# The order and the engines of 1,943 operations, given by two tables of numbers

## The chip, the cores and the metric

The kernel runs on one core of a Trainium2 chip. The metric is the device time of one execution in microseconds; the time of a kernel is the median of several executions. Beside it stands one profiled execution, whose trace gives every duration below. The granted clock of TensorE was 1.0 throughout it.

The engines are named as in the profile: PE is TensorE's matmuls, PEld its weight loads, DVE is VectorE, ACT is ScalarE, POOL is GpSimd, SP is SyncE, whose queue issues most transfers.

## The reference

Two blocks follow each other. The first is attention with routing: every query and key gets the nearest of 16 centroids of its head, and a query attends only to keys of the same centroid. The second is a gated long convolution.

```python
# q, k, v: (4, 8, 768, 64); centroids: (8, 16, 64); all f32
q_assign = np.argmax(np.einsum('bhsd,hcd->bhsc', q_n, c_n), axis=-1)   # k_assign alike
mask = q_assign[:, :, :, None] == k_assign[:, :, None, :]
scores = np.where(mask, scale * np.matmul(q, k.transpose(0, 1, 3, 2)), -1000000000.0)
scores = scores - np.max(scores, axis=-1, keepdims=True)
attn = np.exp(scores)
attn = attn / (np.sum(attn, axis=-1, keepdims=True) + 1e-09)
x = np.matmul(attn, v)                  # -> (4, 768, 512), heads side by side
proj = x @ w_proj                       # (512, 1536)
x1, x2, x3 = (proj[..., :D], proj[..., D:2 * D], proj[..., 2 * D:])
x2_conv = np.fft.irfft(np.fft.rfft(x2, axis=1) * np.fft.rfft(filter_fft, axis=0)[None], n=S, axis=1)
return (x1 * x2_conv * x3) @ w_out      # (4, 768, 512)
```

## The kernel before

**The work.** The 32 pairs of batch and head are taken as 16 pairs of heads. Two pairs make a group n (8 groups, two for each batch element). For each group the kernel loads q and k, transposes them on PE (function `tr` and `tr2`, lines 594 and 607), copies them out of PSUM (line 282 on ACT, 284 on DVE and POOL: one helper, `copy`, serves all), casts them into the operands of the scores (tile `aug`), and works out the masks by a product with the centroids (line 627, or 512 for the first group), maxima and comparisons on DVE and a product with a triangle. The mask rows stand in the same operand tiles as extra rows of the contraction, so that the scores' product (line 84, tiles `aug`) already holds the mask. In the first group, functions named `put` copy the mask rows there on DVE (lines 557 and 284).

For each pair of heads there are six tiles of keys. Each gives three products of scores of 512 columns, three exponentials on ACT (lines 694 and 697), a weighted sum `pv` of eight matmuls (line 708) that accumulates in a PSUM pair, and a running sum of the exponentials for the denominator: line 725 (`part`, 512 columns, DVE or POOL) for the first two tiles, line 729 (`acc`, 1,536 columns, DVE) for the others. The sum over partitions is done by accumulating transfers on POOL's queue, or by a product (line 742) in the first groups and the last. Line 808 divides.

For each batch element the second block follows (`hyena`): the projection of x2 (line 843), sums and differences of its halves (857 and 862), the forward transform as products with a table `fw`, the product with the filter's spectrum (873 and 877), the inverse transform with a table `inv` (function `I`), sums and folds (944 and 954, function `fold`), the other two projections and their product (905 to 917), the gate (959) and the output projection (function `W`). For the last batch element, a sign-changed copy of `inv` is made on ACT (line 881), products of line 959 are split into two halves of the sequence for each of four blocks of columns, output tiles 0 to 2 need the one half and tiles 3 to 5 the other, and the projections of tiles 3 to 5 are split into three quarters of the contraction and the last quarter (that of tile 5 into two halves of its columns besides).

**The order.** No loop fixes the order of instructions. The function `build` lists 1,943 operations with a number (`seq`, in the order of the list), the engines that may run each with a price for every one, a due time, and what each reads and writes. A list scheduler (`place`) then puts them on the engines one by one. For each engine it takes those that are ready, works out when each could start, and of those that could start within 0.1 us of the earliest it takes the one with the least due time. Each operation goes to the engine at which it comes up first. The instructions are issued in the order of the starts that come out of it, and each engine runs its own in that order, waiting by semaphores for what they need. Operations of DVE and POOL marked `lock` (those that read and write SBUF on both) are kept apart: one on POOL waits for the one on DVE that was placed before it.

Two tables steer this. `NUDGE` adds a number to the due time of every operation, and `ONLY` pins an operation to one of its engines:

```python
        o.due += NUDGE.get(o.seq, 0.0)                         # line 99
...
            if o.seq in ONLY:                                  # line 183
                o.eng = {ONLY[o.seq]: o.eng[ONLY[o.seq]]}
...
                c = min((c for c in cand if c[0] <= t0 + wait + 1e-9), key=lambda c: (   # line 212
                    c[1].due - (bonus if e == "PE" and st.kind == "pv" == c[1].kind else 0.0)
```

Tiles in SBUF are held in fixed rings (5 tiles of exponentials, 3 sets of score operands, 4 of raw q and k, 3 of v); eight PSUM banks are given out by the same scheduler, two of them to the weighted sum.

Of the kernel before, what the change touches and what calls it, by code (L numbers as in the profile page):

```python
# [86 lines left out]
class Plan:  # L87
# [6 lines left out]
    def op(self, eng, fn, due, r=(), w=(), alloc=None, free=(), lock=False, byts=0, after=(), kind=None, lat=0.0, tab=None):  # L94
# [3 lines left out]
        o.seq = len(self.ops)  # L98
        o.due += NUDGE.get(o.seq, 0.0)
        o.outs, o.end, o.start, o.on = [], None, None, None  # L100
# [22 lines left out]
    def place(self, free0, banks_for, switch=0.1, wait=0.1, rate=RATE, bonus=0.0, margin=0.02195, shape=0.0):  # L123
# [58 lines left out]
        for o in self.ops:  # L182
            if o.seq in ONLY:
                o.eng = {ONLY[o.seq]: o.eng[ONLY[o.seq]]}
        for o in self.ops:
# [1098 lines left out]
```

## Time and profile before

| what | value |
|---|---|
| median of 3 runs | 371.18 us (371.1 to 372.21) |
| profiled execution | 370.64 us, its span 368.9 us |
| DVE's instructions, ACT's, POOL's | 478, 495, 162 |
| costliest group | line 708, 768 matmuls, busy for 143.0 us |
| DVE's costliest group | line 729, 64 instructions of 1.762 us |
| ACT's costliest group | line 697, 192 exponentials of 0.606 us |
| HBM | 106 GB/s over the span |

The span is the time from the first to the last instruction of the trace; the profiled execution's own time is that and what lies around it. Busy is the time in which an engine has at least one instruction; the idle time that stands with an instruction is that of its engine just before it, with what ended it.

### The profile page before, as it was taken

The page shows a single profiled execution, that of the slowest core. Times are in us where ns is not written, and L with a number is a line of the kernel's source. Part 1 is how long each engine was busy: PE and PEld are TensorE (multiplying, and loading weights), DVE is VectorE, ACT ScalarE, POOL GpSimd, SP SyncE. Part 2 cuts the span into 40 slices and gives each one's busy share as a digit, 9 for nine tenths or more (in the row PEclk, how much of TensorE's full clock was granted, in tenths as well). Part 3 has the DMA queues.
Part 4 walks back from the last instruction along what each step waited for, and adds up shares of the span by engine and source line. Part 5 has one row for each costly group of instructions (what it writes and reads, how often), then busy time and mean ns, then how long its engine had stood idle before and what let it go on. Part 6 is the DMA issues. An engine that isn't in the chain of part 4 may idle for free.

```text
span 368.9 us, 8653 instructions
## 1 busy us (share of the span) xinstructions
PE 357.5 (97%) x3314; PEld 208.9 (57%) x3316; DVE 342.5 (93%) x478; ACT 263.6 (71%) x495; POOL 120.9 (33%) x162
## 2 busy tenths in 40 slices
PE   7899999999999999999999999999999999999985
PEld 4455544555856565565555555566555655566672
DVE  7999999896999899999999999998998999999994
ACT  7998978877986859769869765899584785433242
POOL 7730730422032752331530044352221334016610
PEclk9999999999999999999999999999999999999999
DMA  7986597484247768748556964667477750110124
GB/s 175 202 189 126 128 211 195 93 189 110 62 80 156 115 156 169 152 103 129 107 64 183 238 170 81 146 152 98 81 116 167 150 77 1 48 45 2 59 115 171
DMA packets 90405, 46.20 MB, mean 125 GB/s; under 512 B 78248, under 2 KB 84092, under 8 KB 90364
## 3 DMA queue, kind: packets, MB, share of 16 engines
q1 hardware_dynamic: 85500, 36.15, 40.5%
q0 software_dynamic: 2752, 8.98, 17.1%
q10 hardware_dynamic: 2112, 0.52, 0.6%
q8 instruction: 26, 0.43, 0.5%
q14 instruction: 15, 0.12, 0.1%
HBM read 31.59 MB, written 7.40 MB: 106 GB/s over the span
## 4 chain that ended last, share of the span: by engine, by line
PE 78%; DVE 11%; ACT 5%; issue 3%; DMA 1%; POOL 1%; SPq 0%; DVEq 0%; ACTq 0%; POOLq 0%
PE bank L84 33%; PE pair L708 28%; PE bank L843 5%; PE bank L594 5%; DVE acc L729 3%; PE bank L627 2%; ACT p L697 1%; PE bank L82 1%; DMA qkraw<-in_k_dram 1%; DVE qkP L284 1%; PE bank L475 1%; PE bank L742 1%; ACT p L694 1%; PE bank L607 1%; DVE ohT L655 1%
## 5 line engine op out<-in xcount | busy, mean ns | idle before, releaser
L708 PE MATMUL pair<-p,vraw 128*64 128x385 f32 x768 | 143.0, 489 | 0.1
L697 ACT ACTIVATE p<-bank 128x512 f32<-128x512 f32 x192 | 108.7, 606 | 23.5 <-PE bank L84 16.0
L729 DVE TENSOR_TENSOR acc<-p,acc 128x1536 f32<-128x1536 f32 x64 | 112.8, 1762 | 3.2 <-ACT p L694 0.5
L84 PE MATMUL bank<-aug,aug 80*64 80x512 bf16 (+3 forms) x736 | 81.9, 327 | 2.1 <-ACT p L697 0.9
L708 PEld LDWEIGHTS pair<-p,vraw 128*64 128x64 f32 x768 | 56.6, 136 | 43.8 <-issue 36.7
L84 PEld LDWEIGHTS <-aug 80*64 80x64 bf16 (+1 forms) x736 | 45.6, 109 | 41.0 <-issue 26.3
L694 ACT ACTIVATE p<-bank 128x512 f32<-128x512 f32 x96 | 57.4, 606 | 5.4 <-PE bank L84 3.6
L284 POOL CAST aug<-qkP 64x768 bf16<-64x768 f32 x29 | 25.9, 900 | 83.3 <-DVE acc L729 55.9
L762 POOL DMA_DIRECT2D acc<-acc x30 | 24.4, 824 | 69.8 <-DMA acc<-acc 37.4
L84 PE MATMUL bank<-xT,wpj 128*64 128x384 bf16 x504 | 47.2, 326 | 0.0
L84 PEld LDWEIGHTS <-wpj 128*64 128x64 bf16 x504 | 30.2, 110 | 14.1 <-issue 2.6
L282 ACT COPY qkP<-bank 128x512 f32<-128x512 f32 (+1 forms) x46 | 23.1, 559 | 15.9 <-PE bank L594 9.7
L84 PEld LDWEIGHTS <-y 128*64 128x64 bf16 x472 | 24.0, 110 | 13.2 <-issue 3.6
L725 POOL TENSOR_TENSOR acc<-p,p 128x512 f32<-128x512 f32 x15 | 19.3, 1297 | 32.3 <-DVE acc L729 10.4
L873 DVE TENSOR_TENSOR tm<-bank,hm 128x512 f32<-128x512 f32 x44 | 28.1, 681 | 1.9 <-POOL uv L862 0.8
L84 PE MATMUL bank<-wout,y 128*64 128x512 bf16 (+1 forms) x200 | 24.0, 371 | 1.1 <-DVE y L959 1.1
L282 ACT CAST aug<-qkP 64x768 bf16<-64x768 f32 x28 | 23.2, 830 | 1.0 <-DVE qkP L284 0.4
L843 PE MATMUL bank<-wpj,xT 128*64 128x512 bf16 x192 | 22.7, 379 | 0.4 <-ACT p L697 0.4
L725 DVE TENSOR_TENSOR acc<-p,p 128x512 f32<-128x512 f32 x33 | 21.6, 690 | 0.4 <-DMA dd<-acc 0.4
L877 POOL TENSOR_TENSOR y<-tm 128x512 bf16<-128x512 f32 x14 | 17.8, 1277 | 12.8 <-DVE tm L873 10.6
L732 ACT COPY osb<-pair 128x770 f32<-128x770 f32 x16 | 12.9, 806 | 10.8 <-PE pair L708 10.7
L594 PEld LDWEIGHTS bank<-ident,qkraw 128*128 128x128 f32 x144 | 15.6, 141 | 6.3 <-ACT p L694 2.4
(178 smaller groups left out, 435.7 us busy)
## 6 DMA issues: line engine op xcount, KB each, us to landing
vraw<-in_v_dram SPq DMA_DIRECT2D x16, 384.0 KB, 5.2
qkraw<-in_q_dram SPq DMA_DIRECT2D x30, 192.0 KB, 3.9
rb<-dr SPq DMA_DIRECT2D x30, 192.0 KB, 3.7
qkraw<-in_k_dram SPq DMA_DIRECT2D x28, 192.0 KB, 3.6
out_dram<-ob SPq DMA_DIRECT2D x9, 512.0 KB, 5.0
acc<-acc POOLq DMA_DIRECT2D x10, 384.0 KB, 4.8
acc<-acc POOLq DMA_DIRECT2D x10, 192.0 KB, 4.2
y<-in_moe_filter_fft_dram SPq DMA_DIRECT2D x4, 384.0 KB, 4.3
```

Source lines behind the costliest of these rows:

```text
L84: T.nc.tensor.matmul(out[64 * i:64 * i + 64], lhsT[:, 64 * i:64 * i + 64], rhs, start=start, stop=stop)
L282: T.nc.scalar.copy(out, in_)
L284: (T.nc.vector if e == "DVE" else T.nc.gpsimd).tensor_copy(out, in_)
L594: T.nc.tensor.transpose(bank(h.ids[i // 4])[:, ts(i % 4, 128)], raw(ss[i // NT], i % NT), T.ident[:, ::-1] if 3 <= i < NT else T.ident)
L694: T.nc.scalar.activation(o, ap(h).rearrange("p (a b) -> p a b", a=2), Act.Exp, scale=0.125)
L697: T.nc.scalar.activation(flat(s)[:, lo:lo + 512], ap(h), Act.Exp, scale=0.125)
L708: T.nc.tensor.matmul(o[64 * hp:64 * hp + 64, ch, :385], T.vraw[vs][:, hp, sk * D:(sk + 1) * D], T.p[slots[sk]][:, hp, 384 * ch:384 * ch + ...
L725: alu(e).tensor_tensor(o, x, y, op=Alu.add)
L729: T.nc.vector.tensor_tensor(T.acc[os], T.p[slots[sk]][:, :, :S], T.acc[os], op=Alu.add)
L762: op(("POOL", .8), lambda e, rows=rows: T.nc.gpsimd.dma_start(flat_()[:rows], flat_()[rows:2 * rows], accum_op=Alu.add), te, r=[], w=AK, b ...
L843: T.nc.tensor.matmul(ap(h)[64 * i:64 * i + 64], T.xT[xs][:, kt, c:c + 64], T.wpj[:, kt, DM:2 * DM], start=kt == 0, stop=kt == ND - 1)
L873: op(("DVE", .68), lambda e, i=i, cs=cs, r=r, h=h: T.nc.vector.tensor_tensor(T.tm[r][:, cs], ap(h), hmrow(i, (0, 2, 2, 3)[2 * r + cs]), op ...
```

## The change

The two tables get other numbers; nothing else in the kernel differs. `NUDGE` has 1,943 entries before and after, and all of them differ, by 36.8 us in the median of the absolute differences. `ONLY` has 134 pins before and 128 after: 38 are the same, 28 operations are pinned to another engine, 68 pins are gone and 62 are new. The operations, their transfers, their prices, the tiles and the rule of choice stay as they were; the order and the engines follow from the new numbers, as the scheduler works them out. The diff, cut to some of the entries:

```diff
-NUDGE = {
-29:6.171,51:18.728,52:-22.192,85:-189.385,86:-167.539,89:-195.153,1857:-23.832,
-1886:-370.386,1887:13.072,1888:-296.022,1889:-466.918,1902:-292.682,
-1903:-1955.286,1916:-293.904,1917:-296.037,
...
-ONLY = {
-72:"POOL",100:"DVE",1416:"ACT",1886:"DVE",1926:"SP",
...
+NUDGE = {
+29:-7.972,51:50.833,52:43.343,85:97.767,86:98.143,89:98.42,1857:-129.09,
+1886:-3763.992,1887:-38.825,1888:-1267.888,1889:-13.798,1902:-911.492,
+1903:9.788,1916:-1644.568,1917:30.108,
...
+ONLY = {
+44:"DVE",65:"DVE",72:"ACT",100:"POOL",1416:"DVE",1485:"POOL",1512:"DVE",
+1767:"DVE",1768:"DVE",1819:"ACT",1886:"POOL",1887:"DVE",1926:"ACT",
...
```

In the list, 29 is a load of the first q and k, 44 and 65 a mirror of the angles and a copy of transposed q or k, 51 and 52 a pair of sines, 72 and 100 casts into `aug`, and 85, 86 and 89 three of the four `put`. 1416 and 1819 are copies of the projection of x2, 1485, 1886 and 1887 folds, 1512 a copy of the inverse transform's result, and 1767 and 1768 sums of line 725. 1857 is the sign change of `inv`; 1888, 1902 and 1916 are gates of line 959 for output tiles 0 to 2 (the second to the fourth block of columns), and 1889, 1903 and 1917 those for tiles 3 to 5. 1926 is a store of an output tile. The due time of an operation is the number in the list plus its entry in `NUDGE`.

More of the change, by code (lines that the diff above doesn't have):

```diff
@@ L43 @@
-ONLY = {13:"POOL",14:"POOL",15:"POOL",16:"POOL",18:"POOL",30:"ACT",32:"SP",33:"SP",36:"SP",37:"SP",40:"ACT",41:"DVE",66:"ACT",69:"DVE",72:"POOL",73:"ACT",85:"DVE",86:"DVE",93:"DVE",94:"POOL",97:"DVE",99:"DVE",100:"DVE",101:"POOL",141:"DVE",153:"DVE",213:"ACT",226:"POOL",227:"POOL",233:"POOL",238:"POOL",244:"POOL",245:"DVE",253:"DVE",254:"ACT",257:"DVE",288:"DVE",357:"POOL",358:"DVE",359:"POOL",394:"ACT",404:"ACT",406:"DVE",407:"DVE",408:"POOL",409:"ACT",416:"POOL",417:"POOL",418:"POOL",427:"DVE",430:"ACT",461:"POOL",462:"DVE",463:"DVE",498:"DVE",525:"POOL",533:"POOL",549:"DVE",551:"ACT",555:"ACT",566:"DVE",589:"DVE",593:"POOL",594:"POOL",600:"DVE",604:"DVE",639:"DVE",691:"POOL",692:"ACT",693:"POOL",694:"POOL",696:"ACT",697:"ACT",698:"ACT",699:"POOL",700:"POOL",701:"DVE",711:"DVE",808:"POOL",809:"POOL",856:"DVE",858:"ACT",859:"ACT",861:"POOL",862:"POOL",867:"POOL",913:"DVE",915:"POOL",1002:"DVE",1005:"DVE",1018:"DVE",1067:"ACT",1070:"DVE",1072:"ACT",1075:"ACT",1077:"DVE",1146:"POOL",1147:"POOL",1152:"DVE",1153:"DVE",1154:"POOL",1156:"ACT",1164:"ACT",1168:"ACT",1201:"DVE",1313:"DVE",1315:"ACT",1369:"DVE",1416:"ACT",1421:"ACT",1426:"ACT",1448:"DVE",1457:"DVE",1516:"POOL",1600:"POOL",1601:"POOL",1607:"POOL",1608:"POOL",1609:"POOL",1610:"DVE",1621:"DVE",1812:"ACT",1875:"DVE",1886:"DVE",1919:"ACT",1920:"SP",1922:"DVE",1923:"SP",1926:"SP",1930:"SP",1933:"ACT",1934:"SP",1938:"SP",1942:"SP"}
@@ new lines @@
+ONLY = {14:"POOL",15:"POOL",16:"POOL",18:"POOL",29:"SP",30:"ACT",32:"SP",36:"SP",38:"SP",39:"ACT",40:"ACT",44:"DVE",50:"DVE",65:"DVE",72:"ACT",89:"DVE",93:"DVE",94:"POOL",100:"POOL",101:"POOL",143:"DVE",147:"DVE",149:"ACT",155:"DVE",176:"DVE",177:"POOL",178:"DVE",226:"POOL",227:"POOL",232:"DVE",233:"POOL",238:"POOL",239:"POOL",244:"POOL",253:"ACT",254:"DVE",405:"ACT",407:"DVE",408:"POOL",409:"DVE",410:"ACT",413:"ACT",415:"ACT",416:"ACT",417:"POOL",418:"POOL",429:"DVE",461:"DVE",463:"DVE",498:"ACT",508:"DVE",522:"POOL",524:"DVE",525:"DVE",532:"POOL",548:"DVE",559:"DVE",564:"DVE",570:"ACT",577:"DVE",592:"DVE",600:"DVE",604:"ACT",688:"ACT",689:"ACT",690:"ACT",692:"POOL",693:"ACT",694:"ACT",696:"ACT",699:"POOL",700:"ACT",701:"ACT",857:"DVE",858:"DVE",859:"DVE",861:"DVE",862:"ACT",869:"POOL",870:"ACT",879:"DVE",914:"POOL",915:"POOL",1031:"DVE",1032:"DVE",1047:"DVE",1054:"DVE",1061:"POOL",1067:"DVE",1072:"ACT",1094:"DVE",1095:"POOL",1147:"POOL",1153:"ACT",1154:"DVE",1155:"ACT",1156:"ACT",1164:"ACT",1165:"DVE",1167:"ACT",1168:"DVE",1199:"DVE",1314:"POOL",1315:"ACT",1368:"POOL",1369:"POOL",1416:"DVE",1421:"ACT",1426:"ACT",1448:"DVE",1485:"POOL",1500:"DVE",1512:"DVE",1607:"ACT",1608:"POOL",1622:"DVE",1767:"DVE",1768:"DVE",1819:"ACT",1886:"POOL",1887:"DVE",1909:"ACT",1920:"SP",1923:"SP",1926:"ACT",1933:"ACT",1941:"DVE",1942:"SP"}
```

2 lines of the change are left out of this document (1 added, 1 removed).

## The prediction

> **What bounds the kernel now.** I read the first table of the page, then a table by stretches of 10 us, then the waits of PE, the chain of waits, and the timelines of the first 35 and the last 20 us. The first table says which engines are full; its columns are engine, busy us (share), instructions:
>
> ```profile
> PE 357.5 (97%) x3314; PEld 208.9 (57%) x3316; DVE 342.5 (93%) x478; ACT 263.6 (71%) x495; POOL 120.9 (33%) x162
> ```
>
> PE is the bound and DVE stands close behind it. The table by stretches (stretch, its length, busy us of PE, PEld, DVE, ACT and POOL, then granted clock, DMA share, GB/s) shows where PE is not full:
>
> ```profile
> 0.00:10.00 10.00, 7.44 (x35) 4.08 (x35) 7.36 (x24) 7.34 (x13) 7.16 (x32) 1.00 0.79 177
> ...
> 240.00:250.00 10.00, 9.25 (x108) 6.65 (x104) 9.37 (x14) 9.50 (x18) 5.02 (x5) 1.00 0.68 153
> ...
> 330.00:340.00 10.00, 10.00 (x112) 6.41 (x108) 9.90 (x18) 3.29 (x8) 5.64 (x4) 1.00 0.01 2
> ...
> 350.00:360.00 10.00, 8.93 (x156) 7.08 (x154) 9.85 (x21) 4.29 (x9) 1.40 (x2) 1.00 0.26 107
> 360.00:370.00 10.00, 4.63 (x44) 2.08 (x40) 3.46 (x8) 2.52 (x5) 0.00 (x0) 0.98 0.42 157
> ```
>
> From 30 to 350 us PE's idle time adds up to only 2.5 us (0.66 in 30:40, 0.28, 0.15 and 0.04 in the three stretches from 60, 0.42 in 100:110, 0.05 in each of the two after it, 0.06 in 160:170, 0.75 in 240:250). But ends of matmuls are modelled, so busy hides short stalls. I therefore also added up columns: unhindered, eight matmuls of the weighted sum (line 708) start 1.295 us apart, and a pair of 512-column half matmuls 0.213. At those rates the matmuls between 30 and 350 us fill 303 of the 320 us, so 17 are lost there; 10.7 are lost before 30 us and 6.2 between 350 and 368.9. Those 34 us are all that another order can work on. Part of the 17 is this, in the chain of waits (start, us, what):
>
> ```profile
> 79.71 1.30 PE pair L708 x8
> 81.00 1.47 PE bank L594 x12
> 82.47 1.45 PE pair L708 x8
> ```
>
> The weighted sum costs 1.45 behind the transposes (full-width array) and 1.30 behind the half-array scores. The matmuls change the width of their array tiles 59 times; at 0.10 to 0.15 each that is 6 to 9 of the 17 us, and 8 to 11 are short stalls.
>
> The end of the kernel, in the timeline (start, us, engine, line, operation, count, idle time before it and what ended it):
>
> ```profile
> 356.92 1.00 POOL L954 TENSOR_TENSOR sim<-sd 128x384 f32<-128x384 f32 x1 [6.52 <-DVE sd L944]
> ...
> 359.22 5.41 PE L84 MATMUL bank<-wout,y 128*64 128x256 bf16 x54 [1.07 <-DVE y L959]
> ...
> 361.88 0.55 DVE L959 TENSOR_TENSOR y<-sim,qkP 128x384 bf16<-128x384 f32 x1
> ...
> 364.67 0.69 DVE L284 COPY ob<-bank 128x512 f32<-128x512 f32 x1 [1.90 <-PE bank L84]
> ```
>
> PE waits for a gated product (line 959), then runs nearly the whole output projection in one piece; the last product is ready at 362.43, PE ends at 364.63, and a copy and a store take the last 4.3 us.
>
> At the front, DVE builds the first masks without a break from 14.65 to 22.79, ACT is full from 14.42 to its table load, and the first exponential waits 0.41:
>
> ```profile
> 21.02 1.28 ACT L408 ACT_TABLE_LOAD   x1
> ...
> 22.93 0.60 ACT L697 ACTIVATE p<-bank 128x512 f32<-128x512 f32 x1 [0.41 <-PE bank L84]
> ```
>
> **The change part by part.** No operation is added or removed. All 1,943 due times move, by a median of 37 us in either direction. The kernel compares due times only among operations that could start within 0.1 us of the earliest, so most of these shifts decide nothing by themselves. The engine pins can be read directly. I matched them to the engine each operation ran on (the placement agrees with the trace: 29 casts of line 284 on POOL, 28 on ACT, 7 on DVE). 60 pins name another engine than before; 68 old pins go, and 35 of those operations had run on DVE.
>
> *Engine load.* At the rows' means (cast 0.54 DVE, 0.83 ACT, 0.90 POOL; 512-column copy 0.69 DVE, 0.59 ACT; line 725 sum 0.69 DVE, 1.30 POOL; mask step 0.55 DVE, 0.48 ACT; fold 0.55 DVE, 1.01 POOL) the 60 moves add 6.1 us to DVE and take 2.9 from ACT and 2.5 from POOL. DVE has 26.4 idle. The 35 freed operations can move the other way; their mean price on DVE is near 0.6, so a third of them leaving would give 7 back. I set the net at nothing, with bounds of minus 6 and plus 6 us of DVE work.
>
> *Front, before 35 us.* One first q/k load (due 6.5 to -7.7) is pulled ahead in SP's queue, past two others at about 0.65 us of issue each, which come that much later. Before the first score a mirror and a q/k copy go from ACT to DVE, a cast from POOL to ACT and a cast from DVE to POOL: DVE +0.56+0.55-0.54 = +0.57, ACT -0.51-0.49+0.83 = -0.17. ACT's last pair of sines (1.0 us, at 13.36) gets due times of 52 and 60 where it had -13 and 27, so it falls behind the casts and copies; the exponential's table load needs it, and the total ahead of the load stays the same. PE waits 0.9 for a load and 0.7 for a copy here, and 0.41 end before the first exponential: a gain of up to 2.0. A loss of up to 1.1, if two DVE instructions of 0.55 get ahead of the mask copies, whose due times rise from -180 to 107. I take **-0.5**, nearer the row of the shortest wait, because both engines have to get shorter for the first exponential to move.
>
> *Middle, 35 to 350 us.* The waits with a name are few: 0.9 us of PE for exponentials (three times), 0.7 for a mask, 1.05 lost in 246 to 248 us, where scores wait for exponentials behind a 0.87 us sign change of the inverse table on ACT. That one instruction gets a due time 105 us earlier (258 to 153), out of the way of a full ACT (9.50 of 10 in 240:250). Bounds: 0 to -4 from stalls, half of the 8 lost; +3 if half of DVE's 6.1 lands where DVE has no gap. I take **-1.2**: that stall and a little of the others.
>
> *End.* Output tiles 3 to 5 have their last quarter split off (0.22 us of PE each, half that for the two halves of tile 5); tiles 0 to 2 do not. Before, the products for tiles 0 to 2 had due times of 45 to 50 for the last three column blocks and came last, so four quarter-blocks and whole projections, 2.2 us, stood behind the last product. Now they get -569 to -1301, and the products for tiles 3 to 5 327 to 374. If those come last, 0.22+0.22+0.11+0.11 = 0.66 us of PE remains behind the last product: a gain of up to 1.5. One fold goes from DVE to POOL and another back; on POOL it costs 1.00 against 0.55, so 0.45 are lost if it stands in that chain. One store goes from SP's queue to ACT's, ahead of at most one copy; ACT waits 1.90 to 2.83 between copies there, which hides its issue (0.33), and it costs 0.33 without that cover. Bounds -1.5 and +0.6; I take **-1.0**, the gain less that 0.45.
>
> For the fold on POOL the row has 6.52 us of idle time ended by DVE. "SBUF — State Buffer" (Who interferes with whom) of the Trainium skill says that a DVE instruction with two SBUF inputs and a GpSimd instruction that reads SBUF shut each other out. The trace agrees as far as that row goes; by this rule the handover costs up to one more 0.55 us DVE instruction, and the end would be -0.45 instead of -1.0.
>
> *Sum.* -0.5 - 1.2 - 1.0 = -2.7. The profiled execution took 370.64 us (span 368.9 and 1.74 around it), so 367.94 for such a one; the median of the three runs is 0.54 above it, which gives **368.5 us**.
>
> **The rivals.**
> *A larger gain.* The front reaches its 2.0, the end its 1.5 and the middle 2: 371.2 - 5.5 = 365.7. For it: 34 us are lost in all. Against: DVE's chains at both ends keep their length. 0.15.
> *Nothing.* The stalls reappear elsewhere, since PE's work and the operations between the first load and the first exponential are the same: 371.2. 0.13.
> *DVE becomes the bound (slower).* After 290 us DVE is 9.6 to 10.0 of 10 busy, and the pins after 280 add: a tile copy 0.69, two sums 1.38, a copy 0.55, less a fold 0.55 and a copy 0.69, net +1.4. If the freed pins do not take that away, and the front and end gain nothing, the end comes at 371.2 + 1.4 = 372.6. It decides once DVE's queue, and not PE's, is what holds 300 to 350: idle time on PE there, ended by lines 873 or 917. Against: PE is at 10.00 there and had slack of one or two tiles. 0.16.
> *More changes of the array (slower).* Ten more than 59, at 0.15, with no gain elsewhere: 371.2 + 1.5 = 372.7. For it: the due times of transposes and scores lose their old grouping. Against: nothing shows that they get more scattered. 0.06. "TensorEngine Tiling (Array Packing)" (Key Properties) of the Trainium skill says that a change of tiling mode drains the engine; the 1.45 against 1.30 agrees.
>
> **How the numbers follow.** Forecast 0.50, larger gain 0.15, nothing 0.13, DVE 0.16, array 0.06. About 0.3%, or 1.1 us, is what a measurement here can tell from no change, so same means 370.1 to 372.3. Faster: 0.50 + 0.15 = 0.65, slower: 0.16 + 0.06 = 0.22, same 0.13. The likeliest case alone spans 367 to 370. The range reaches to the larger gain and to both slower rivals: 365.6 to 372.7.
>
> **What would show it.** In the changed profile: PE's busy time within 1 us of 357.5 and its idle time lower by 2 to 3; the first exponential between 21 and 23 us; no stall of PE near the sign change of the table (line 881); less than 1 us of PE behind the last product of line 959. It is wrong if PE shows idle time ended by DVE after 300 us, if the first exponential is later than 24, or if PE's busy time rises by over 1.5 us, which would be the array's changes.

## The result, and the profile after

The changed kernel takes 374.27 us in the median of 6 executions (373.12 to 375.03), the kernel before 371.12 beside it (370.98 to 372.21). The ratio is 1.0078, with a 95% interval of 1.0055 to 1.0101: slower by about 3 us, where 2.7 less was forecast, and 1.6 us above the upper end of the range. The profiled execution took 374.13 us, its span 372.4.

The first table of the page of the changed kernel (engine, busy us, share, instructions):

```profile
PE 361.2 (97%) x3319; PEld 215.0 (58%) x3319; DVE 340.0 (91%) x470; ACT 272.6 (73%) x509; POOL 116.3 (31%) x156
```

DVE is busy for 2.5 us less than before, PE for 3.7 more. The matmuls are the same (a few of their records are missing in either trace: 3,314 and 3,319 are there), and counted as in the prediction the array changes its width 59 times, as before. So the 3.7 us are not work. PE's idle time is 372.4 - 361.2 = 11.2 us, against 368.9 - 357.5 = 11.4: the whole lengthening stands inside what the page calls busy. From 30 us on both traces show a bf16 matmul of 512 columns as 0.38 us long (0.40 at most), while the next pair can start 0.21 us behind it; a start that comes up to 0.17 us late therefore leaves no idle time. The stretches show the same (stretch, its length, then PE, PEld, DVE, ACT, POOL, clock, DMA share, GB/s):

```profile
0.00:10.00 10.00, 8.83 (x35) 4.51 (x35) 7.09 (x24) 6.80 (x13) 7.12 (x41) 1.00 0.74 167
...
240.00:250.00 10.00, 9.99 (x118) 7.07 (x115) 9.55 (x12) 9.31 (x19) 1.59 (x2) 1.00 0.38 75
250.00:260.00 10.00, 9.48 (x83) 6.05 (x84) 8.54 (x13) 9.42 (x20) 4.39 (x4) 1.00 0.73 104
...
350.00:360.00 10.00, 10.00 (x154) 7.36 (x152) 9.60 (x20) 4.37 (x9) 3.25 (x4) 1.00 0.14 54
360.00:370.00 10.00, 6.99 (x80) 3.58 (x74) 6.85 (x15) 3.84 (x8) 0.69 (x1) 1.00 0.50 190
```

In the first 10 us PE is "busy" for 1.39 us more, with the same 35 matmuls. Most of that is not the new order. The first matmuls of every execution (line 1096) start 0.43 us apart and are shown as 0.63 us long, later ones of the same line start 0.22 apart and take 0.38, although the granted clock reads 1.00. How many are slow differs from execution to execution: 7 in the profile before and 11 after, but also 12 in e7_relief and 11 in e17_rsum, which leave the front of the kernel before untouched and have the first exponential at 23.03 and 23.04 us (before 22.93). PE's busy time from 0 to 30 us is 27.38 and 27.21 us in those two and 26.36 before, so a difference of 1 us in busy time can come from this alone.

What can be compared is the **lag**: the time t, less what the matmuls that have started by t would take unhindered, at the rates of the prediction. In us, from one profiled execution each (the kernels named e… are the experiments below; e16_again is the changed kernel itself, profiled once more):

| kernel | 100 | 160 | 176 | 200 | 220 | 240 | 260 | 350 | PE ends |
|---|---|---|---|---|---|---|---|---|---|
| before | 15.97 | 19.45 | 20.25 | 21.30 | 21.57 | 22.72 | 24.98 | 27.67 | 364.63 |
| after | 16.72 | 20.10 | 21.83 | 23.01 | 23.44 | 24.58 | 26.88 | 30.11 | 368.07 |
| e16_again | 16.50 | 20.53 | 21.28 | 23.09 | 24.47 | 25.61 | 27.77 | 31.15 | 368.92 |
| e2_put | 16.50 | 19.91 | 20.64 | 22.80 | 23.07 | 24.22 | 26.52 | 30.09 | 368.06 |
| e5_mask | 16.13 | 19.55 | 20.37 | 21.79 | 22.94 | 24.08 | 26.38 | 29.61 | 367.58 |
| e6_cast | 16.20 | 19.60 | 20.34 | 21.36 | 21.75 | 22.90 | 26.11 | 29.34 | 367.31 |
| e14_sum | 16.09 | 19.72 | 20.46 | 21.48 | 22.18 | 23.34 | 25.64 | 28.87 | 366.60 |
| e8_rev | 15.84 | 19.06 | 19.87 | 21.74 | 22.38 | 23.58 | 25.73 | 28.59 | 365.99 |
| e15_rload | 16.07 | 19.59 | 20.89 | 21.82 | 22.11 | 23.26 | 25.40 | 28.12 | 365.08 |
| e17_rsum | 16.05 | 19.51 | 21.83 | 23.30 | 23.99 | 25.08 | 27.16 | 30.00 | 367.52 |

One profile is one execution: kernels whose PE order is the same up to 160 us differ there by up to 0.5, and the two profiles of the changed order differ by 0.55 at 176 us and by 1 us from 220 us on. Smaller differences than these are not read from the table. In its first profile the changed kernel is behind by 0.75 at 100 us (the front), 0.65 at 160, 1.58 at 176, 1.86 at 240, 1.90 at 260, 2.44 at 350 and 3.44 at PE's end.

**Front.** ACT's timeline (start, us, engine, line, operation, idle before): the fourth mask copy `put` now runs on ACT ahead of the table load, and the first exponential starts at 24.19, 1.26 us later.

```profile
21.85 0.80 ACT L555 ACTIVATE aug<-bank 16x768 bf16<-16x768 bf16 x1
22.67 1.28 ACT L408 ACT_TABLE_LOAD   x1
...
24.19 1.08 ACT L697 ACTIVATE p<-bank 128x512 f32<-128x512 f32 x2
```

**170 us.** The chain of waits has a load of q in it that SP (SyncE's queue) issues only 6.9 us before PE transposes it; PE waits 0.9 us:

```profile
163.82 6.73 DMA qkraw<-in_q_dram
170.55 0.14 issue
170.69 1.57 PE bank L594 x12
```

The trace marks the completion of each load in sixteen parts. Fifteen parts of this one had landed by 167.49 us; PE waited for the sixteenth, at 170.55. In e16_again, the same kernel, all sixteen had landed by 167.89 and PE did not wait. So this wait belongs to some executions of the changed order and not to all.

**250 us.** The stall at 246 to 248 is gone, and one at 250 has come. The timelines of PE after, and then before:

```profile
250.45 1.29 PE L84 MATMUL bank<-aug,aug 128*64 128x512 bf16 x8 [0.46 <-ACT p L697]
```

```profile
247.29 0.89 PE L84 MATMUL bank<-aug,aug 128*64 128x512 bf16 x4 [0.47 <-ACT p L697]
```

Between 240 and 260 the lag grows by 2.30 us after and by 2.26 before: the stall moved and kept its size.

**End.** The fold on POOL, PE's last waits, DVE's last product and its last copy:

```profile
359.69 1.00 POOL L954 TENSOR_TENSOR sim<-sd 128x384 f32<-128x384 f32 x1 [6.37 <-DVE sd L944]
...
361.52 0.88 PE L84 MATMUL bank<-wout,y 128*64 128x512 bf16 x4 [0.36 <-DVE y L959]
363.05 5.02 PE L84 MATMUL bank<-wout,y 128*64 128x512 bf16 x50 [0.65 <-DVE y L959]
...
365.97 0.56 DVE L959 TENSOR_TENSOR y<-sim,qkP 128x384 bf16<-128x384 f32 x1
...
368.01 0.42 DVE L284 COPY tm<-bank 128x256 f32<-128x256 f32 x1 [1.48 <-PE bank L84]
```

The products for tiles 0 to 2 come first now, as read from the due times. PE has 368.07 - 366.53 = 1.54 us behind the last product, not 2.20; but the last product itself is 4.1 us later, more than PE's lag explains.

### The profile page after: what moved, and what is told of

The parts are those of the page before. It is cut to its first block, busy times and chain, and to the rows that moved or that the text cites. A ratio compares the mean times of both kernels' runs of the same rounds, so it can differ in the third digit from the quotient of the medians.

```text
span 372.4 us, 8630 instructions
## 1 busy us (share of the span) xinstructions
PE 361.2 (97%) x3319; PEld 215.0 (58%) x3319; DVE 340.0 (91%) x470; ACT 272.6 (73%) x509; POOL 116.3 (31%) x156
## 4 chain that ended last, share of the span: by engine, by line
PE 81%; DVE 6%; ACT 6%; issue 2%; DMA 2%; POOL 0%; SPq 0%; ACTq 0%; POOLq 0%; DVEq 0%
PE bank L84 33%; PE pair L708 31%; PE bank L843 5%; PE bank L594 4%; PE bank L627 2%; DMA qkraw<-in_q_dram 2%; ACT p L697 2%; DVE acc L729 1%; ACT p L694 1%; PE bank L607 1%; PE bank L475 1%; PE bank L742 1%; PE bank L512 1%; PE bank L82 1%; ACT aug L282 1%
## 5 line engine op out<-in xcount | busy, mean ns | idle before, releaser
L729 DVE TENSOR_TENSOR acc<-p,acc 128x1536 f32<-128x1536 f32 x64 | 113.1, 1767 | 2.8 <-ACT p L697 0.6
L84 PE MATMUL bank<-aug,aug 80*64 80x512 bf16 (+3 forms) x742 | 84.5, 327 | 1.5 <-ACT p L697 1.1
L708 PEld LDWEIGHTS pair<-p,vraw 128*64 128x64 f32 x768 | 59.3, 136 | 40.3 <-issue 33.3
L84 PEld LDWEIGHTS <-aug 128*64 128x64 bf16 (+1 forms) x742 | 47.9, 109 | 38.7 <-issue 26.3
L284 POOL CAST aug<-qkP 64x768 bf16<-64x768 f32 x20 | 19.3, 965 | 70.1 <-DVE acc L729 20.7
L282 ACT COPY qkP<-bank 128x512 f32<-128x512 f32 (+1 forms) x49 | 25.0, 552 | 17.0 <-PE bank L594 9.3
L282 ACT CAST aug<-qkP 64x768 bf16<-64x768 f32 x35 | 28.8, 830 | 1.7 <-PE bank L84 1.0
L725 DVE TENSOR_TENSOR acc<-p,p 128x512 f32<-128x512 f32 x34 | 24.5, 741 | 1.0 <-ACT p L697 0.9
L877 POOL TENSOR_TENSOR y<-tm 128x512 bf16<-128x512 f32 x15 | 18.9, 1276 | 17.7 <-DVE tm L873 12.2
L725 POOL TENSOR_TENSOR acc<-p,p 128x512 f32<-128x512 f32 x14 | 17.9, 1302 | 19.7 <-ACT od L282 6.6
L282 ACT COPY ob<-bank 128x512 f32<-128x512 f32 x21 | 12.2, 591 | 10.9 <-PE bank L84 8.3
## 6 DMA issues: line engine op xcount, KB each, us to landing
qkraw<-in_q_dram SPq DMA_DIRECT2D x30, 192.0 KB, 4.1
rb<-dr SPq DMA_DIRECT2D x30, 192.0 KB, 3.5
qkraw<-in_k_dram SPq DMA_DIRECT2D x28, 192.0 KB, 4.1
acc<-acc POOLq DMA_DIRECT2D x10, 192.0 KB, 4.3
```

What stands on the lines that cost most here:

```text
L84: T.nc.tensor.matmul(out[64 * i:64 * i + 64], lhsT[:, 64 * i:64 * i + 64], rhs, start=start, stop=stop)
L282: T.nc.scalar.copy(out, in_)
L284: (T.nc.vector if e == "DVE" else T.nc.gpsimd).tensor_copy(out, in_)
L708: T.nc.tensor.matmul(o[64 * hp:64 * hp + 64, ch, :385], T.vraw[vs][:, hp, sk * D:(sk + 1) * D], T.p[slots[sk]][:, hp, 384 * ch:384 * ch + ...
L725: alu(e).tensor_tensor(o, x, y, op=Alu.add)
L729: T.nc.vector.tensor_tensor(T.acc[os], T.p[slots[sk]][:, :, :S], T.acc[os], op=Alu.add)
```

## The experiments

Four theories stand in the expectations. **A**: the changed order leaves no margin at a few places, and their costs add up. **B**: PE falls back to some late chain whatever is repaired. **C**: steps of POOL and DVE that stretch each other are the cause. **D**: late loads of q and k are.

All edits but one work on the finished order. `shift(seqs, ahead_of)` moves operations in it, `on` changes an operation's engine. The kernel before took 370.70 to 370.89 us in the median of each set. Ratios are to it.

**The tail alone.** The numbers of the changed kernel for the 103 operations that come last in it, in the kernel before; up to 334 us the order stays that of before.

```diff
+# in NUDGE and ONLY: the changed kernel's entries for the 103 operations that it starts last
```

> The kernel before with the changed kernel's due times and pins for the 103 operations that stand last in the changed kernel's order; up to 334 us it issues what the kernel before issues, and from there what the changed kernel does. Theory A with a third of the loss at the end: the last product of line 959 comes 1 us later relative to the rest, 372.1. If the end of the changed kernel is as good or better, as the prediction had it (0.66 us of PE behind the last product instead of 2.2): 370.2 to 371.1.

e4_tail: 371.56 us, ratio 1.0017 (1.0007 to 1.0026). The tail costs 0.6 us where it was to bring 1.0. PE in e4_tail, the two last groups:

```profile
359.24 0.88 PE L84 MATMUL bank<-wout,y 128*64 128x512 bf16 x4 [0.36 <-DVE y L959]
360.76 5.03 PE L84 MATMUL bank<-wout,y 128*64 128x512 bf16 x50 [0.65 <-DVE y L959]
```

PE's last unbroken run of about 5 us starts at 360.76. Before it started at 359.22, 1.54 us earlier, with one wait ahead of it in place of two. Not all of this is the tail's: the profiled execution was the slowest of the eleven, and DVE is 0.70 us late in it already at 336 us (line 857's sums begin at 336.97, before at 336.27), where both kernels still have the same order. About 0.8 us are left for the tail. DVE is full there (9.85 of 10 before) and its products decide; the new order of them gives PE the ones it needs later. In that order DVE waits 0.37 us for a copy on ACT, and three of the last gates stand directly behind the fold that they read and start 0.58 to 0.59 us after it, where other neighbours on DVE start 0.46 to 0.48 apart; that makes some 0.7 us.

**The front.** In e1_const the copy of line 459 goes behind the first mask copies; in e2_put the fourth mask copy goes back to DVE.

```diff
+    shift([157], 248); shift([158, 160], 168)            # e1_const, in the changed kernel
+    o = next(x for x in order if x.seq == 88)            # e2_put, in the changed kernel
+    o.on = "DVE"; shift([88], 85)
```

> The changed kernel with one DVE copy (line 459, the reversed identity, 0.73 us) and the two half-array products that read it (line 462) moved behind the first mask copies; nothing else moves. Theory A (the loss is made of a few local stalls, and one of them is at the front: two constants' casts, 0.67 and 0.73 us, stand among the copies of q and k that the first masks need): first exponential at 23.4 to 23.7 instead of 24.2 us, time 0.5 to 0.8 less than the changed kernel's 374.3, so about 373.6. Theory B (the loss is spread: ACT carries 9 us more and exponentials come late all along, so a repair at one place is taken back at the next): first exponential earlier, but 374.3 as before.

> The changed kernel with the one mask copy that had gone to ACT (line 555, 0.80 us, just ahead of the table load for the exponentials) put back on DVE. Theory A: table load at 21.8 instead of 22.67, first exponential near 23.4, 0.5 to 0.8 less than 374.3. If DVE's longer chain of four mask copies is what holds the scores instead, the first exponential stays near 24 and the time at 374.3. Theory B: 374.3 in either case.

The first exponential came at 23.01 and 23.66 us; the times are 374.12 (1.0077, 1.0058 to 1.0097) and 374.23 (1.0095, 1.0076 to 1.0114), no gain. At 160 us e2_put is only 0.19 us ahead of the changed kernel's first profile, at 176 us 1.19; 0.89 of that is the wait at 170 us, which this execution does not have. At 200 us 0.21 are left. Its chain of waits says why (SPq is a transfer being issued on SP):

```profile
190.99 0.65 SPq L497
...
191.68 0.91 SPq L497
...
192.63 0.59 SPq L497
...
193.26 3.82 DMA aug<-ohT
```

The masks of the group at 190 us go out by small transfers on SP, when DVE and ACT have made them, and PE waits 0.7 us for one. That chain does not get earlier because PE does.

**The masks.** e5_mask has both front edits and undoes four changes of engine at 178 to 184 us: a fold (line 954) and a gate (959; the expectations call it the last step of a state update) go back from DVE to POOL, two mask steps (655) from DVE to ACT (653). e8_rev does the reverse in the kernel before, and nothing else.

```diff
+    on = {593: "POOL", 594: "POOL", 1165: "ACT", 1168: "ACT", 88: "DVE"}   # e5_mask, with e1's and e2's shifts
+    shift([594], 1129); shift([1168], 1164); shift([1165], 1201)
+    on = {593: "DVE", 594: "DVE", 1165: "DVE", 1168: "DVE"}                # e8_rev, in the kernel before
+    shift([1165], 1167)
```

> The changed kernel with both front repairs together (the L459 copy behind the first mask copies, the fourth weight copy on DVE) and, new, the chain that makes the masks of the group at 190 us relieved on DVE: the fold and the last step of one state update (L954, L959) go from DVE to the idle POOL, and two of the four mask steps (L655 on DVE) go to ACT as L653, as in the kernel before. Theory A (the changed order leaves no margin at a few places, and each repair counts once the next place is repaired too): the mask DMAs start at about 186.5 us instead of 189, no wait of PE for a mask at 195, 21.3 to 21.9 us lost by PE at 200 us (changed kernel 23.0), time 373.0 to 373.4 us. Theory B (PE falls back to some other late chain whatever is repaired): the loss reappears by 260, time 374.0 to 374.3 us.

> The kernel before with the changed kernel's engines for one stretch: the fold and last step of the state update at 178 us on DVE in place of POOL, and two of the four mask steps at 184 us on DVE in place of ACT. Nothing else. Theory A: the mask DMAs at 188 us start 1 to 2 us later and PE waits for a mask at 195 by 0.4 to 1.3 us, time 371.4 to 372.2 us. Theory B (no cost by itself): 370.8 to 371.2 us.

e8_rev: 372.2 us, ratio 1.0046 (1.0034 to 1.0058). SP's masks and PE's weighted sum behind the scores that need them, before and then in e8_rev:

```profile
187.89 6.12 SPq L497 DMA_DIRECT2D aug<-ohT  x8
...
196.58 1.47 PE L708 MATMUL pair<-p,vraw 128*64 128x385 f32 x8
```

```profile
189.53 6.08 SPq L497 DMA_DIRECT2D aug<-ohT  x8
...
197.46 1.49 PE L708 MATMUL pair<-p,vraw 128*64 128x385 f32 x8
```

The masks go out 1.64 us later and PE is 0.88 later. That is theory A, at this place. Not all of the 1.4 us is lost here: the lag of e8_rev is 0.38 below that of the kernel before at 176 us, 0.44 above it at 200, and PE ends 1.36 later; where the rest is lost was not followed. e5_mask: 373.61 us, 1.0078 (1.0066 to 1.009), no gain that can be told. Its lag at 200 us is 1.22 below that of the changed kernel's first profile, at 220 only 0.50. A cast on POOL had moved beside DVE's sums; POOL and DVE there:

```profile
195.72 4.80 POOL L284 CAST aug<-qkP 64x768 bf16<-64x768 f32 x1
```

```profile
195.49 1.74 DVE L729 TENSOR_TENSOR acc<-p,acc 128x1536 f32<-128x1536 f32 x1
197.16 1.00 DVE L808 SCALAR_TENSOR_TENSOR xT<-osb,rb 128x768 bf16<-128x768 f32 x1
198.09 4.05 DVE L729 TENSOR_TENSOR acc<-p,acc 128x1536 f32<-128x1536 f32 x2
```

The cast takes 0.82 alone. e6_cast (below) has the same edits up to 240 us. In its profile POOL begins this cast 1.27 us earlier, ahead of the sums; it takes 0.82, and the lag grows by 0.39 between 200 and 220 us, in e5_mask by 1.15. So about a microsecond on POOL decides this from one execution to another.

**The stall at 246 or 250 us.** e6_cast, in the changed kernel, is e5_mask with three casts moved from ACT to POOL. e7_relief takes the sign change of line 881 and a cast out of ACT's full stretch, in the kernel before. e11_masks6, also in it, makes the masks of that group earlier.

```diff
+    on = {1599: "POOL", 1600: "POOL", 1602: "POOL"}                        # e6_cast, on e5_mask
+    on = {1602: "POOL"}; shift([1857], 1493)                               # e7_relief, in the kernel before
+    shift([1018], 1385); shift([1332, 1335], 1035)                         # e11_masks6, in the kernel before
+    shift([1599, 1602], 1680); shift([1049], 1542); shift([1857], 1482)
```

> The kernel before with the sign change of line 881 (ACT, 243.5 us, first read by PE after 345) moved to an idle stretch of ACT near 320 us, and ACT's cast at 244.4 us (first read after 280) moved to POOL. This is the step of the prediction that was worth most in the middle, alone. Theory A: PE's waits of 0.7 us at 246 to 248 and about 1 us of loss there are gone, and as the rest is the kernel before, it stays gone: 370.0 to 370.5 us. Theory B: lost again further on, 370.8 to 371.2 us.

> As e5_mask, and three of ACT's casts at 246 us (2.4 us together, first read after 280) go to POOL, which waits there. Theory A: the exponentials at 249 start some 2 us earlier, the 0.5 us wait of PE for L697 at 250 and the 0.9 us lost there are gone, time 0.5 to 0.9 us below e5_mask, 372.1 to 372.8 us. Theory B: PE waits for the masks of that group or for DVE instead, time as e5_mask.

> The kernel before, for its own loss at 240 to 250 us (1.8 us), which e7_relief left untouched although ACT then stood idle there. Reading: five scores fill the free banks and PE waits for the round through the exponentials, and the scores cannot start earlier since their masks land just then. So: the routing of that group goes ahead of a state step on DVE (0.95 us) and the four mask steps together on ACT, two casts and the sign change leave that stretch of ACT, and a filter product of 0.8 us goes between the scores. If that reading is right: the scores start 0.5 to 1 us earlier, PE's waits of 0.7 us for L697 are gone, 370.0 to 370.5 us. If the round through ACT is bound otherwise: 370.7 to 371.2 us.

e7_relief: 371.16 us, 1.0015 (1.0007 to 1.0023), no gain. ACT and PE in it:

```profile
246.80 0.60 ACT L697 ACTIVATE p<-bank 128x512 f32<-128x512 f32 x1 [1.00 <-PE bank L84]
```

```profile
247.44 0.90 PE L84 MATMUL bank<-aug,aug 128*64 128x512 bf16 x4 [0.46 <-ACT p L697]
```

ACT now stands idle for 1.00 us ahead of that exponential, waiting for PE's scores, and PE still waits its 0.46 after them. The sign change beside the stall was not its cause: PE waits for the exponentials of scores that it has itself only just made. e11_masks6 got to 371.06 (1.0007, 0.9999 to 1.0016); its masks came earlier, the wait of 0.5 stayed and another of 0.9 for a copy on ACT came, so that guess for the remedy fell too. e6_cast, 374.08 (1.0096, 1.0078 to 1.0113), is the instructive miss: level with the kernel before at 240 us (lag 22.90 and 22.72), it loses 3.21 by 260, where the casts on POOL stretch two of DVE's folds from 0.55 to 0.85 and 1.17 and PE then waits 1.18 for what follows them on DVE.

**The loads.** e3_qload issues the two late loads ahead of a v load; e13_load issues them 9 us earlier, ahead of the masks; e15_rload makes them late in the kernel before.

```diff
+    shift([895, 897], 1140)     # e3_qload, in the changed kernel
+    shift([895, 897], 885)      # e13_load, in the changed kernel
+    shift([895, 897], 1094)     # e15_rload, in the kernel before
```

> The changed kernel with the two loads of raw q and k that SP issues at 163.8 and 164.5 us put ahead of the load of v (384 KB, issued at 162.7) and of the store of the denominators behind it, that is about 1 us earlier. Theory A: the 0.89 us in which PE waits for that q at 170 us goes, and 0.6 to 0.9 of the time: about 373.5. Theory B: the wait goes, but the time stays within 0.3 of 374.3 because exponentials or DVE are late next.

> The changed kernel with one edit: the last two q and k loads of the tile that PE transposes at 170.7 us are issued ahead of the eight mask DMAs (at about 154.5 us) and not behind them (163.8 and 164.5), where SP stood waiting for the masks anyway. The kernel before issues these two some 30 us ahead. Theory D (the changed order issues its q and k loads so late that their landing, 4 to 6.7 us, decides, and varies from run to run): the wait of 0.9 us at 170.7 is gone, the slow executions of 374.4 to 375 us grow fewer, median 373.0 to 373.5 us. Theory B (something else holds the clock): 374.1 us.

> The kernel before with those two loads issued as late as in the changed kernel: behind the masks and behind the store and load of the denominators, at about 165 us in place of 135 to 141 us. Theory D: PE waits 0.5 to 1.5 us for a q or k load at 170.8 us, median 371.3 to 372.3 us, with a wider spread than before. Theory B: no change, 370.8 us.

> The changed kernel itself, unedited, beside the other three on the same chip. All theories: 373.6 to 374.4 us; with a spread of 1.5 to 2 us among its executions, as at first.

e3_qload: 376.41 (1.015, 1.0127 to 1.0173), worse by 2 us; the masks of the group at 190 us came 2 us later still (last transfer issued at 194.92, then 4.28 to land), and the traces show why. The store of the denominators (`dd<-acc`) now stands behind both loads. SP issues it at 164.97 us and not at 163.44; fifteen of its sixteen parts have landed by 168.88, the last at 169.89. The next sum on DVE writes an `acc` tile anew and waits for that. DVE in the changed kernel, and then in e3_qload:

```profile
167.46 0.68 DVE L725 TENSOR_TENSOR acc<-p,p 128x512 f32<-128x512 f32 x1
```

```profile
170.01 0.69 DVE L725 TENSOR_TENSOR acc<-p,p 128x512 f32<-128x512 f32 x1 [2.55 <-DMA dd<-acc]
```

DVE is late by 2.55 us there and still by 2.07 at 184.87, where it begins the masks.

e16_again: 374.45 (1.0084, 1.006 to 1.0108). e13_load: 374.89 (1.0091, 1.0068 to 1.0113): alone it gains nothing. In its profile the wait at 170 is gone, but PE had waited at 121 us already:

```profile
121.01 1.51 PE L594 MATMUL bank<-ident,qkraw 128*128 128x128 f32 x12 [0.96 <-ACT p L697]
```

The exponential named there had ended at 120.72. What ended last was another load of q, issued at 112.23 and landed at 120.92. That load goes out as the third of five loads of q and k between 109 and 116 us (before there are three, the last issued at 110.7; all have landed by 115.7, and PE transposes at 118.35). In the profiles of the changed order and its edits (us):

| | e18_fold | e10_coll | after | e2_put | e1_const | e9_all | e16_again | e13_load |
|---|---|---|---|---|---|---|---|---|
| q load issued | 111.65 | 112.02 | 112.24 | 112.04 | 111.86 | 111.66 | 112.18 | 112.23 |
| landed | 117.79 | 118.42 | 118.72 | 119.31 | 120.13 | 120.23 | 120.28 | 120.92 |
| PE transposes | 119.57 | 119.89 | 120.12 | 119.90 | 120.22 | 120.32 | 120.37 | 121.01 |
| PE waited | 0 | 0 | 0 | 0 | 0.60 | 0.77 | 0.40 | 0.96 |

None of these edits touches that load. It takes 6.1 to 8.7 us, and from a landing at 120.1 on PE starts 0.09 us behind it. That is theory D at another place than the one repaired; no run moves this load. e15_rload: 372.07 in the median, ratio 1.0023 (1.0006 to 1.0041). Its profile is of its fastest execution; the lag at 176 us is 20.89 in place of 20.25, and PE waits for the second of the two loads:

```profile
172.16 0.87 PE L594 MATMUL bank<-ident,qkraw 128*128 128x128 f32 x6 [0.29 <-DMA qkraw<-in_k_dram]
```

So theory D holds in the kernel before, with 0.9 us (0.2 to 1.5 by the interval). The wider spread that it expected is not shown: 371.1 to 373.46 us, against 370.58 to 372.89 for the kernel before beside it. In the changed kernel only one of two late places was repaired.

**POOL beside DVE.** e10_coll takes three POOL steps away from DVE's sums in the changed kernel; e9_all does that and all repairs so far but for the loads; e12_rcoll puts two of them on POOL in the kernel before; e18_fold adds one to e14_sum below.

```diff
+    on = {607: "DVE", 1063: "DVE", 1316: "ACT"}; shift([1316], 1296)   # e10_coll, in the changed kernel
+    shift([1599, 1600, 1602], 1618)                                    # e9_all: e5_mask, e10_coll and this
+    on = {607: "POOL", 1063: "POOL"}                                   # e12_rcoll, in the kernel before
+    on = {1063: "DVE"}                                                 # e18_fold, on e14_sum
```

> The changed kernel with only the three POOL steps of e9_all moved off POOL; front, masks and casts as changed. Theory C (the stretching of DVE by POOL steps, 0.4, 0.7 and 1.6 us in the trace of the changed kernel, is the cause): DVE's stretched instructions at 192 and 269 us are gone, time 372.5 to 373.2 us. Theory A: DVE gets shorter at places where PE does not wait for it: 373.8 to 374.3 us.

> The changed kernel with all repairs before 300 us: those of e5_mask, ACT's three casts of 246 us moved to an idle stretch of ACT near 276 us in place of POOL, and three steps of POOL that were seen to stand beside DVE instructions with both inputs in SBUF (a state fold at 190 us, a cast at 196 us, the last step of a state update at 269 us) on DVE, ACT and DVE. Theory A (short margins at a few places, the sum of them is the loss ahead of the tail): 21.3 to 21.8 us lost at 200 us, 24.9 to 25.6 at 260, 28.2 to 28.9 at 350 (before 27.7, changed 30.1), time 372.2 to 372.9 us; what is left of the difference is the tail, which cost 0.6 alone. Theory B: 374 us again. Theory C (POOL and DVE steps that stretch each other are the whole cause): as A here.

> The kernel before with two DVE steps put on POOL as in the changed kernel: the state fold at 189 us and the last step of the state update at 271 us. It tells what a POOL step beside DVE's sums over the exponentials costs. Theory C: both stretch (POOL's fold from 1.0 to 2 us or more, a DVE sum from 0.68 or 1.75 by 0.5 to 1.6 us), time 371.2 to 372.0 us. Theory A: the stretch is seen, but PE does not wait for it: 370.7 to 371.1 us.

> e14_sum with one more step off POOL: the last step of the state update at 268 us goes to DVE (0.96 us), since in e14_sum it stretched a DVE sum there from 0.69 to 2.31 us. Theory A: DVE gains 0.7 us at 268 to 271 us, and PE a part of it only if it waits for DVE there, which its trace does not show: 372.5 to 372.9 us. Theory C: 372.0 to 372.4 us.

e10_coll: 374.34 (1.0101, 1.0083 to 1.012). The stretched sums at 192 and 269 us are gone from its trace, and the time is not shorter: theory C falls as the whole cause. Such sums are not new either: the kernel before has two, at 133.9 and 187.7 us, 0.84 and 0.34 us longer than their like. e18_fold: 373.0 (1.0059, 1.0046 to 1.0073), no gain on e14_sum either. e9_all: 373.73 (1.0088, 1.0068 to 1.0108), with executions from 373.33 to 375.53; the profiled one was the longest, and waits 0.77 us for the load at 120 and 1.46 for the one at 171. e12_rcoll: 372.61 (1.0048, 1.0036 to 1.0061). Put where DVE sums, the two POOL steps cost the kernel before 1.8 us, most of it at the second (its lag is 0.2 us above that of the kernel before at 260 us and 1.5 at 300); POOL and PE there:

```profile
272.05 3.39 POOL L959 TENSOR_TENSOR y<-yy,x 128x768 bf16<-128x768 f32 x1 [3.04 <-DVE acc L725]
```

```profile
275.50 0.41 PE L84 MATMUL bank<-wout,y 128*64 128x512 bf16 x2 [1.06 <-POOL y L959]
```

It takes 3.39 us where its like take 1.83, and PE waits 1.06 for it.

**All together.** e14_sum is e5_mask, the early loads of e13_load, and the cast that POOL stretched on ACT at 222 us. e17_rsum puts three pieces into the kernel before: the tail, e8_rev's engines and e15_rload's loads.

```diff
+    on = {1316: "ACT"}; shift([1316], 1296); shift([895, 897], 885)     # e14_sum, on e5_mask
+    shift([1165], 1167); shift([895, 897], 1094)                        # e17_rsum, on e4_tail, with e8_rev's engines
```

> e13_load with the repairs of e5_mask (front and masks of the group at 190 us), and the cast that POOL stretched to 4.8 us there on ACT at 222 us. Theories A and D together: 21.2 to 21.6 us lost at 200 us, 21.5 to 21.9 at 220, 28.5 to 29.0 at 350, median 372.4 to 372.9 us, of which 1 us above the kernel before is the tail. Theory B: 373.6 us or more, as e5_mask.

> The kernel before with three pieces of the changed one put in together: the tail (e4_tail), the engines of the stretch at 178 to 184 us (e8_rev) and the two late loads (e15_rload). If the pieces add up: 0.6 + 1.4 + 0.9 = 2.9 us above the kernel before, 373.4 to 374.0 us, with a spread like the changed kernel's. If they hide each other (the late load and the late masks lie 15 us apart): 372.2 to 372.8 us.

e14_sum: 372.88 (1.0046, 1.003 to 1.0063), 1.57 us less than e16_again in the same set, so the repairs together give back about half of what the changed order lost. e17_rsum: 373.53 (1.0064, 1.0051 to 1.0078): the three pieces make 2.4 us by the ratio, of the 3 or so of the changed order. Alone they made 0.6, 1.7 and 0.9 by their ratios, 3.2 in all, so they add up in the main and not fully; by the medians it is 2.8 of 3.3, and 373.53 lies in the range expected for pieces that add up. Its lag runs like the changed kernel's (the table: 21.83 at 176, 30.00 at 350), and PE ends at 367.52 against 368.07. Its wait for the second of the late loads:

```profile
173.10 0.88 PE L594 MATMUL bank<-ident,qkraw 128*128 128x128 f32 x6 [0.41 <-DMA qkraw<-in_k_dram]
```

PE waited 0.86 us ahead of 171.84 too. The profile puts that down to an exponential, but the first of the two loads had landed at 171.71, 0.13 us ahead of PE's start, as in the changed kernel (170.55 and 170.69).

No version ran faster than the kernel before.

## Why the prediction was wrong, step by step

The prediction failed at its sum. It added up gains from waits that it could name in the old profile and took a loss in only one part at a time: the upper end of its range, 372.7, is one rival alone. Its own bounds for losses (+1.1 in front, +3 in the middle, +0.6 at the end) make 375.9 together, and losses in all three parts came.

**Front, -0.5: wrong sign.** The first exponential came 1.26 us later, and the lag at 100 us is 0.75 higher. The step weighed waits that could end (up to 2.0) against two DVE instructions that might get ahead (1.1), and took the lighter side; what happened is of the second kind: a cast and a copy of constants (lines 1061 and 459, 1.4 us together) stand on DVE among the first q and k copies, and a 0.80 us mask copy went onto ACT. That this reaches the end is not shown: the repairs of the front alone gave nothing.

**Middle, -1.2: wrong.** The stall was read by its neighbour. The sign change left the stretch from 240 to 250 us (it starts at 239.16, before at 243.51), the stall went elsewhere with its size, and e7_relief shows that it does not hang on it. The bound of +3 for losses was thought of as DVE work, but DVE's work fell by 2.5 us. The losses that came are of margins, that is, of the time by which something is ready ahead of its use: loads issued 6 to 8 us ahead of their use (the two at 170 us, issued more than 20 us ahead in the kernel before, cost 0.9 us when put there late), and a chain of masks that goes through a full DVE (1.4 us when put there). The prediction compared engine loads and named waits of the kernel before. It had no term for a wait that only the new order makes, although "half of the stalls" was taken off for those that it ends.

**End, -1.0: wrong, 0.6 the other way.** That less of PE stands behind the last product was right (1.54 in place of 2.20, not 0.66). The term left out is the chain of DVE: with the tail alone the products themselves came 1.1 us later (the last one ended at 364.24, before at 362.43, less the 0.70 by which that execution was late already). The fold on POOL took 1.00 as in the row. The 6.52 us of idle time in that row say nothing of a handover: the fold reads what line 944 writes on DVE, and waits for that. The handover weighed by the Trainium skill ("SBUF — State Buffer", Who interferes with whom) was not paid there: beside the fold, at 359.69 to 360.69 us, DVE's instructions (lines 917 and 954) each had an input in PSUM. One reading of the step was wrong without weight in its sum: ACT waits 1.53, 2.83 and 0.49 us between its last copies before; the 1.90 given for it is DVE's.

**Rivals.** The array's changes stayed at 59. "DVE becomes the bound" named the right side and the wrong sign of the load: DVE has less to do, and PE's waits after 300 us are for the gate (1.0 us, as before), not for lines 873 or 917. DVE holds PE in two short chains, the masks at 180 to 190 us and the products of the last 12 us.

**What would show it.** The first exponential beyond 24 us did show it. PE's idle time did not (11.2 against 11.4), and a rise of PE's busy time was put down to the array in advance. The rise came, 3.7 us, but the array changed its width 59 times as before: it was stalls too short to show as idle time, and up to 1 us of it can be the slow matmuls at the start.

**What stays open.** The three pieces of e17_rsum make about 2.4 of some 3 us. e14_sum is still 1.7 us slower than the kernel before by its ratio; 0.6 of that is the tail, the rest has no run that places it. Why a repair alone gave nothing in the changed kernel is read from one trace each, and not shown by a run of its own: e2_put's gain goes into the masks, e5_mask's into POOL's cast, e3_qload's into DVE's wait for the store; e1_const, e9_all and e13_load wait for the load at 120. The changed order scatters by up to 2 us between executions; that the loads at 120 and 170 make the most of it fits the profiles (waits of 0 to 0.96 and 0 to 1.46 us there), but no run took both away and measured the spread.

## What to carry to other kernels

A new order of the same work can use up margins that no engine's load and no named wait of the old profile shows: before trusting a gain of that kind, look at how long ahead of its use each load and each small transfer is issued, before and after, and compare with the spread of its landing. Read a stall by what happens when its neighbour is taken away, not by who stands next to it. And where PE is near full, compare columns streamed against time: its busy share hides what it waits for. Profile the same kernel twice before reading a difference of less than 1 us: here two profiles of one order were 1 us apart.

## What the runs showed of the hardware that was not expected

How long a small transfer takes to land differs between two orders of the same work. The 60 mask transfers of line 497, from issue to landing, before and then after:

```profile
DMA to landing us min/median/max: 1.8/2.4/3.9
```

```profile
DMA to landing us min/median/max: 1.8/3.2/5.4
```

The load of q took 6.73 us at 170, and the one at 112 us between 6.1 and 8.7 from profile to profile, where the median of such loads in the changed kernel's trace is 4.1. What makes the difference at 170 is one of sixteen parts: fifteen were there after 3.67 us. In e9_all, where PE waited 1.46 us at the same place, fifteen parts of that load had landed by 168.72 us and the last at 171.30.

In the changed kernel 27 times an instruction of line 873 on DVE, with one input in PSUM, ran beside a step of line 877 on POOL, and none was longer than alone (0.68 us). All four of DVE's instructions in that trace that took over 0.25 us more than their like (at 35.7, 169.0, 192.0 and 269.0 us) are sums of lines 725 and 729, with both inputs in SBUF, beside a step of POOL. The Trainium skill ("SBUF — State Buffer", Who interferes with whom) says that such a DVE instruction and a GpSimd one that reads SBUF contend and that the later one waits for the whole of the other; the traces agree: the sum at 269.02 us starts 0.04 us behind POOL's step of 1.82 and takes 1.64 longer than its like. What went beyond the estimate of one more instruction: the POOL cast in e5_mask, shown above, let three DVE instructions pass (those at 195.49, 197.16 and 198.09) and took 4.8 us for 0.82.
